# Two buffers for the combine weights of a fused attention, soft-MoE and MLP kernel, and three expert matrices loaded in halves during attention

## The chip, the cores and the metric

The kernel runs on one core of a Trainium2 chip. The metric is the device time of one execution in microseconds (us); the median of the runs shown is what a change is judged by. A core has five engines with an instruction queue each: TensorE (PE, matmuls; its weight loads are listed apart as PEld), VectorE (DVE), ScalarE (ACT), GpSimd (POOL) and SyncE (SP). Here SP issues every transfer between DRAM and on-chip memory; the transfers themselves run on the core's 16 DMA engines. Each engine takes its instructions strictly in the order in which they were written, so an instruction that waits holds up all that stands behind it on that engine.

## The reference

Three layers on 4608 tokens of width 512 (8 batches of 576 tokens, 8 heads of 64), all in fp32.

```python
# 1 attention inside chunks of 64 tokens
scores = scale * q_c @ k_c^T ; attn = softmax(scores) ; x = attn @ v_c      # -> x [4608, 512]
# 2 soft mixture of experts: 8 experts x 4 slots = 32 slots
logits = x @ phi                                    # [4608, 32]
d = softmax over the 4608 tokens ; slot_input = d.T @ x
h = relu(slot_input[e] @ w1[e]) ; slot_out[e] = h @ w2[e]    # w1[e] 512x1024, w2[e] 1024x512
c = softmax over the 32 slots                       # the combine weights
y = c @ slot_out                                    # [4608, 512]
# 3 MLP
out = softplus(y @ w_in) @ w_out                    # 512 -> 2048 -> 512
```

The kernel multiplies slot_out by w_in first (a table of 32 x 2048), so the hidden layer of the MLP is c times that table.

## The kernel before, in words

**Stages.** Attention comes first (to about 174.7 us of the profiled span). It works in 36 units, each two heads of 512 tokens: SP loads q and k of a unit (step `lq`, two transfers of 256 KB) and v for two units (`lv`, four of 128 KB), PE transposes q and k (L404), forms the scores (L435), transposes them (L468), multiplies by v (L487) and transposes the result (L522); DVE, ACT and POOL evict and scale in between. There are three buffers for q and k, so the loads of a unit are issued when the unit three before it has been transposed. Then come the experts: sixteen `H` steps of PE (L931) multiply the slot inputs by the halves of w1 (1 MB each), sixteen `SO` steps (L973) multiply by the halves of w2. Meanwhile the combine weights are prepared, and the first quarter of w_in and of w_out is converted from the words in which they are held to the number form that PE takes. Then the table is built (`Td`, L1013), and 72 quarter tiles of the MLP follow (`h` L1084, softplus on DVE and ACT, `o` L1142 to L1146) to the end.

**Combine weights.** They are made in three batches of 1536 tokens. For each: `c1` on PE transposes logits; `c20`, `c21` on DVE subtract the row maximum into a tile `cc` (L816); `c3` on ACT takes the exponential (L820); `c40` to `c42` on DVE divide by the row sum (L826 to L831); `c5` on ACT writes the high part into a tile `cr` (L839); `c6` on POOL writes the low part (L843); three `d` steps on PE transpose `cr` (L850), and three `dc` steps on DVE or ACT copy the result into the table `cT` (L856). The tiles `cc` and `cr` have one buffer each: the second batch may write `cc` only when `c6` of the first has read it. They lie where attention's expert buffers d0 to d4 were, so the first `c21` also waits for the `H` step that reads d2.

**Weight conversion.** A piece of 512 columns goes through `cb0`, `cb1`, `cb2` on DVE (L335, L338, L342), a copy and a square on ACT (L347, L350; the square lies between `cb1` and `cb2`) and a sum `cg` on POOL (L872). Pieces of w_out are then split once more (`ch` L879, `cl` L883). Four pieces of w_in and the first two of w_out stand on DVE ahead of the step `so0` (L983), which scales the first half of the experts' result; `so1` on ACT does the other half, and PE's L992 (`soT`) needs both.

**Loads.** SP's queue is in order. The sixteen halves of w1 lie in slots w0, w1, g0 to g2, d0 to d4, w2 to w6, g3 (in the order of the `H` steps); the d slots are free only when attention's buffers are closed. The halves of w2 come into i0 to i3 and w7, and then into slots that `H` or `SO` steps have left. A transfer takes one of eight semaphores in turn and waits for the transfer eight before it, so at most eight are in flight.

**Order.** A planner (`issue`) writes the instructions out. Every step has an engine, a cost, a rank and the steps and buffers that it needs; the planner keeps a clock per engine and always writes the step that could start first. Its costs set the order, not the time. Steps given the engine None cost nothing and are written as soon as what they stand behind is written. While it waits for the last two halves of w2, PE multiplies something that nothing reads (`fill`, L914).

```python
FILL = {("SO", 14): 4, ("SO", 15): 3, ("o", 0): 2}          # lost matmuls ahead of these steps
add("c21", b, ..., [("c20", b)] + start_, [("cc", b)], ...)  # takes a buffer cc
add("c6", b, ..., [("c5", b)], (), [("cc", b)], r)           # gives it back
bufs.update({"mt": 4, "cv": 4, "cc": 1, "cr": 1, ...})
```

Of the kernel before, what the change touches and what calls it, by code (L numbers as in the profile page):

```python
# [8 lines left out]
F32 = mybir.dt.float32  # L9
U32 = mybir.dt.uint32  # L10
F32R = mybir.dt.float32r
# [6 lines left out]
LAG = 3  # L18
BUSY = 36
WAIT = 0  # L20
FILL = {("SO", 14): 4, ("SO", 15): 3, ("o", 0): 2}


# [2 lines left out]
W2 = ["i0", "i1", "i2", "i3", "w7", "w0", "w1", "w2", "w3", "w4", "w5", "w6", "g3", "i0", "i1",  # L26
      "i2"]
# [117 lines left out]
def kernel(  # L145
# [12 lines left out]
    nc = tc.nc  # L158
# [127 lines left out]
    def load(nm, n, sl):  # L286


        e, i = divmod(n, 2)
        if nm == "w1":  # L290
            src = moe_w1[e].rearrange("(p k) f -> p k f", k=4)[:, 2 * i:2 * i + 2]
        elif nm == "w2":
            src = moe_w2[e, i * 512:(i + 1) * 512, :].rearrange("(p b a) f -> p b (a f)", b=2, a=2)
        else:
            src = w_out_u[256 * n:256 * n + 256, :].rearrange("(k p) f -> p k f", p=128)
        parts = halves(sl)
        if sl[0] == "w":
            for t, x in zip(parts, (src[:, 0], src[:, 1])):
                nc.sync.dma_start(out=t.bitcast(U32) if nm == "wo" else t, in_=x)
        else:  # L300
            t = V["slot", sl]
            t = (t.bitcast(U32) if nm == "wo" else t).rearrange("p (b f) -> p b f", b=2)
            for x in (slice(0, 1), slice(1, 2)) if nm == "w2" and n >= 14 else (slice(0, 2),):
                nc.sync.dma_start(out=t[:, x], in_=src[:, x])
        if nm == "w2":
            parts = [t.rearrange("p (a f) -> p a f", a=2) for t in parts]
        wt[nm, n] = parts

    def load_wi(c, pr):
        src = w_in_u[256 * pr:256 * pr + 256, 1024 * c:1024 * c + 1024].rearrange(  # L310
# [307 lines left out]
    def add(nm, key, fn, deps=(), take=(), give=(), rank=0.0, cost=None, after=()):  # L618
        s = Step(nm, key, fn, [by[d] for d in deps if d in by], take, give, rank, cost,
                 [by[d] for d in after])  # L620
        by[nm, key] = s
        steps.append(s)
# [96 lines left out]
    def at(f, *a):  # L719
        return lambda e, held: f(*a)  # L720

    for n, sl in enumerate(W1):
        if sl[0] != "d":
            add("lw", ("w1", n), at(load, "w1", n, sl), rank=100 + n)
    for n in range(5):
        add("lw", ("w2", n), at(load, "w2", n, W2[n]), rank=130 + n)
    ends = ((raw_ctx, "A1", ["d0"]), (qk_ctx, "S", ["d1", "d2"]), (v_ctx, "D", ["d3", "d4"]))
    deps = []
    for i, (c, nm, sls) in enumerate(ends):
# [79 lines left out]
    def st_c2(b, step, e, held):  # L809
        p = V["c", b]  # L810
        if step == 0:
            V["cm"] = st_p.tile([128, NC, 1], F32, tag="cm", name="cm", bufs=1)
            nc.vector.tensor_reduce(out=V["cm"], in_=p, axis=AX.X, op=ALU.max, negate=True)
        else:
            c = V["c", b] = K["keep"].tile([128, NC, NS], F32, tag="cc", name="cc")
            nc.vector.tensor_tensor(  # L816
                out=c, in0=p, in1=V["cm"].to_broadcast([128, NC, NS]), op=ALU.add)

# [16 lines left out]
        return x.unsqueeze(2).to_broadcast([128, NC, 2, NS])  # L835

    def st_c5(b, e, held):
        cr = V["cr", b] = K["keep"].tile([128, NC, 2, 2, NS], F32R, tag="cr", name="cr")
        nc.scalar.copy(out=cr[:, :, :, 0], in_=two(V["c", b]))  # L839

    def st_c6(b, e, held):
# [518 lines left out]
    held = {(sl, "w1"): 0 for sl in W1 if sl[0] != "d"}  # L1360
    held.update({(W2[n], "w2"): 0 for n in range(5)})
    bufs = {sl: 0 for sl in W1 + W2 if sl[0] != "d"}
    bufs.update({"mt": 4, "cv": 4, "cc": 1, "cr": 1, "ph": 2, "scr0": 1, "scr1": 1, "scr2": 1, "hold": 0})
    held.update({("hold", f"{j}{h}"): 2 * j + i for j in range(4) for i, h in enumerate("ab")})
    for i, k in enumerate(late):
        by["cb0", k].after = [by["o", (EARLY + 2 + 3 * i // 2, 0)]]
# [49 lines left out]
```

## Time and profile before

| | us |
|---|---|
| three runs | 678.26, 678.83, 678.56 (median 678.56) |
| the profiled execution's own time | 677.97 |
| its span, first to last instruction | 676.2 |
| attention, to the last step ahead of the experts | 174.7 |
| experts, combine weights and first conversions, to `so0` | 174.7 to 226.9 |
| table and MLP | 226.9 to 676.2 |
| busy: PE, DVE, ACT, POOL | 634.6, 430.2, 318.0, 237.8 |

The profile is of one execution, whose own time lies 1.8 above its span. A row of the timeline gives start, length, engine, line, operation, what is written from what, how many, and in brackets how long the engine stood idle before it and who released it. A row of SP's queue (SPq) gives when a transfer is issued, not when it lands. Names as trm, sops, hps and ph are PE's result tiles; g, i, w and d are weight slots.

### The profile page before, as it was taken

The page shows a single profiled execution, that of the slowest core. Times are in us where ns is not written, and L with a number is a line of the kernel's source. Part 1 is how long each engine was busy: PE and PEld are TensorE (multiplying, and loading weights), DVE is VectorE, ACT ScalarE, POOL GpSimd, SP SyncE. Part 2 cuts the span into 40 slices and gives each one's busy share as a digit, 9 for nine tenths or more (in the row PEclk, how much of TensorE's full clock was granted, in tenths as well). Part 3 has the DMA queues.
Part 4 walks back from the last instruction along what each step waited for, and adds up shares of the span by engine and source line. Part 5 has one row for each costly group of instructions (what it writes and reads, how often), then busy time and mean ns, then how long its engine had stood idle before and what let it go on. Part 6 is the DMA issues. An engine that isn't in the chain of part 4 may idle for free.

```text
span 676.2 us, 14087 instructions
## 1 busy us (share of the span) xinstructions
PE 634.6 (94%) x5849; PEld 511.6 (76%) x5849; DVE 430.2 (64%) x631; ACT 318.0 (47%) x478; POOL 237.8 (35%) x205
## 2 busy tenths in 40 slices
PE   5899899878995899999999999999999999999997
PEld 4688678756454677888788788888888888888885
DVE  1678778765237799878887877754555554545551
ACT  2566457543126587734554755544333333333330
POOL 4233233220114536613222233444433344433341
PEclk7999999998897999999999999999999999999999
DMA  9799889899999903112313510222414223231412
GB/s 169 195 245 275 234 235 287 212 300 413 416 409 411 391 5 128 59 63 93 125 63 118 195 62 32 79 78 79 110 62 125 63 85 103 78 110 63 121 35 62
DMA packets 80543, 107.93 MB, mean 160 GB/s; under 512 B 42464, under 2 KB 60896, under 8 KB 78560
## 3 DMA queue, kind: packets, MB, share of 16 engines
q1 hardware_dynamic: 80480, 107.04, 49.0%
q8 instruction: 46, 0.75, 0.5%
q14 instruction: 17, 0.14, 0.1%
HBM read 88.15 MB, written 18.87 MB: 158 GB/s over the span
## 4 chain that ended last, share of the span: by engine, by line
PE 81%; DVE 8%; issue 4%; ACT 3%; POOL 2%; DMA 1%; SPq 1%; POOLq 0%; DVEq 0%; ACTq 0%
PE trm L1146 18%; PE trm L1144 18%; PE trm L1142 18%; PE ph L1084 5%; PE tr L404 4%; PE X L487 3%; PE S L435 2%; PE hps L931 2%; PE tr L468 2%; PE tr L522 2%; PE tr L540 2%; PE tr L598 1%; DMA q<-in_q_dram 1%; DVE nm L446 1%; DVE ph L1113 1%
## 5 line engine op out<-in xcount | busy, mean ns | idle before, releaser
L1123 POOL TENSOR_TENSOR g<-hTm,g 128x1024 fp32r<-128x1024 f32 (+1 forms) x37 | 86.8, 2348 | 105.1 <-ACT g L1119 101.5
L1109 ACT ACTIVATE hTm<-hTm 128x1024 f32<-128x1024 f32 (+2 forms) x51 | 51.4, 1010 | 79.8 <-DVE hTm L1103 79.6
L1103 DVE TENSOR_SCALAR hTm<-ph 128x1024 uint32<-128x1024 uint32 (+2 forms) x51 | 59.0, 1158 | 34.6 <-PE ph L1084 34.5
L421 POOL COPY T<-T 64x512 f32<-64x512 f32 x72 | 44.0, 611 | 104.3 <-ACT T L413 103.5
L1113 DVE SCALAR_TENSOR_TENSOR hTm<-ph,hTm 128x1024 f32<-128x1024 f32 (+1 forms) x37 | 44.1, 1193 | 23.5 <-ACT hTm L1109 23.4
L1119 ACT CAST g<-hTm 128x1024 fp32r<-128x1024 f32 (+1 forms) x37 | 37.9, 1025 | 41.0 <-DVE hTm L1113 41.0
L1158 DVE TENSOR_TENSOR i<-trm,i 128x512 f32<-128x512 f32 x52 | 35.7, 686 | 32.0 <-PE trm L1146 31.8
L413 ACT COPY T<-tr 128x512 f32<-128x512 f32 x72 | 40.9, 588 | 29.5 <-PE tr L404 29.4
L1084 PEld LDWEIGHTS ph<-cT,Tc 128*128 128x128 f32 x288 | 43.6, 190 | 10.1 <-issue 2.8
L1084 PE MATMUL ph<-cT,Tc 128*128 128x256 f32 x288 | 47.0, 286 | 0.8 <-DVE ph L1113 0.7
L1103 DVE TENSOR_SCALAR siT<-ph 128x1024 uint32<-128x1024 uint32 (+1 forms) x25 | 29.5, 1180 | 26.0 <-PE ph L1084 26.0
L1123 POOL TENSOR_TENSOR g<-siT,g 128x1024 fp32r<-128x1024 f32 x12 | 28.9, 2407 | 42.8 <-ACT g L1119 42.8
L1109 ACT ACTIVATE siT<-siT 128x1024 f32<-128x1024 f32 (+1 forms) x25 | 25.7, 1026 | 36.8 <-DVE siT L1103 36.6
L1123 DVE TENSOR_TENSOR g<-ph,g 128x1024 fp32r<-128x1024 f32 (+2 forms) x27 | 29.7, 1102 | 11.9 <-ACT g L1119 11.9
L446 DVE TENSOR_REDUCE nm<-S 128x8 f32<-128x512 f32 x36 | 24.7, 686 | 18.9 <-PE S L435 18.8
L404 PE MATMUL tr<-ident,q 128*128 128x128 f32 x144 | 29.8, 290 | 6.3 <-DMA q<-in_q_dram 5.2
L1119 ACT CAST g<-ph 128x1024 fp32r<-128x1024 f32 (+2 forms) x27 | 24.9, 922 | 19.5 <-DVE ph L1113 18.1
L435 PEld LDWEIGHTS S<-T 64*64 64x64 f32 x1152 | 21.1, 137 | 16.1 <-issue 12.5
L435 PE MATMUL S<-T 64*64 64x64 f32 x1152 | 25.4, 225 | 7.5 <-issue 2.5
L404 PE MATMUL tr<-ident,k 128*128 128x128 f32 x144 | 28.9, 283 | 2.2 <-issue 2.2
L460 ACT ACTIVATE P<-P 128x512 f32<-128x512 f32 x36 | 23.0, 638 | 11.5 <-DVE P L452 11.4
L452 DVE TENSOR_TENSOR P<-S,nm 128x512 f32<-128x512 f32 x36 | 24.5, 679 | 2.1 <-PE S L435 1.3
(439 smaller groups left out, 1748.4 us busy)
## 6 DMA issues: line engine op xcount, KB each, us to landing
part<-i SPq DMA_DIRECT2D x18, 512.0 KB, 2.6
i<-part SPq DMA_DIRECT2D x18, 512.0 KB, 3.7
q<-in_q_dram SPq DMA_DIRECT2D x32, 256.0 KB, 4.7
k<-in_k_dram SPq DMA_DIRECT2D x32, 256.0 KB, 4.4
vbm<-in_v_dram SPq DMA_DIRECT2D x40, 128.0 KB, 4.2
g<-in_moe_w_dram SPq DMA_DIRECT2D x5, 1024.0 KB, 7.6
d<-in_moe_w_dram SPq DMA_DIRECT2D x5, 1024.0 KB, 12.1
i<-in_moe_w_dram SPq DMA_DIRECT2D x5, 1024.0 KB, 15.2
```

The lines of the kernel that those rows point to most:

```text
L404: nc.tensor.transpose(c, t[:, h, 2 * rr:2 * rr + 2, :].rearrange("p r d -> p (r d)"), ident)
L421: nc.gpsimd.tensor_copy(out=t[a:a + 64, :, 1], in_=t[b:b + 64, :, 2 * h])
L435: nc.tensor.matmul(out=sp[64 * o:64 * o + 64, b, 64 * i:64 * i + 64], lhsT=cs[:, 0], rhs=cs[:, 1], start=True, stop=True)
L1084: nc.tensor.matmul(out=ph(n, a, b)[:, j - a, :], lhsT=K["Tc"][:, f * 128:(f + 1) * 128], rhs=K["cT"][:, t * TT:(t + 1) * TT], start=True, ...
L1103: nc.vector.tensor_scalar(out=scratch(n, a, b).bitcast(U32), in0=ph(n, a, b).bitcast(U32), scalar1=0x80000000, scalar2=None, op0=ALU.bitwi ...
L1109: nc.scalar.activation(out=y, in_=y, func=AF.Softplus)
L1113: nc.vector.scalar_tensor_tensor(out=soft(n, a, b), in0=ph(n, a, b), scalar=0.0, in1=y, op0=ALU.max, op1=ALU.add)
L1119: nc.scalar.copy(out=V["gs", n][:, 0, a:b], in_=soft(n, a, b))
L1123: tt(e)(out=s[:, 1, a:b], in0=soft(n, a, b), in1=s[:, 0, a:b].bitcast(F32), op=ALU.subtract)
L1142: nc.tensor.matmul(out=po, lhsT=s[:, 0, j, ts_], rhs=wr[:, hs], start=(n in begin and j == 0), stop=False)
L1144: nc.tensor.matmul(out=po, lhsT=s[:, 0, j, ts_], rhs=wr[:, ls], start=False, stop=False)
L1146: nc.tensor.matmul(out=po, lhsT=s[:, 1, j, ts_], rhs=wr[:, hs], start=False, stop=(j == 3 and n in finish))
```

## The change

Two things are edited. The tiles `cc` and `cr` get two buffers each. And three halves of w1, number 10, 11 and 12 of the `H` steps (slots w2, w3, w4), are no longer loaded after attention's last loads but in six parts of 512 KB, each written into SP's queue right behind the q and k loads of one unit: units 8, 10, 12, 21, 26 and 31. The old load steps stay in the planner as empty ones, so that it plans as before. The same is done with the first five halves of w2 (i0 to i3, w7): they now stand in the queue right behind the load of g3, ahead of d0 to d4 instead of behind them.

```diff
+EARLY_LOADS = {10: (8, 10), 11: (12, 21), 12: (26, 31)}
...
+    def load_half(n, sl, i):
+        src = moe_w1[n // 2].rearrange("(p k) f -> p k f", k=4)[:, 2 * (n % 2) + i]
+        if i == 0:
+            wt["w1", n] = halves(sl)
+        nc.sync.dma_start(out=wt["w1", n][i], in_=src)
...
+    def ahead(key, f, step):
+        add("ld", key, f, cost={None: 0.0}, after=[step])
+
     for n, sl in enumerate(W1):
         if sl[0] != "d":
-            add("lw", ("w1", n), at(load, "w1", n, sl), rank=100 + n)
+            add("lw", ("w1", n), at(lambda: None) if n in EARLY_LOADS else at(load, "w1", n, sl),
+                rank=100 + n)
+        for i, u in enumerate(EARLY_LOADS.get(n, ())):
+            ahead((n, i), at(load_half, n, sl, i), ("lq", u))
     for n in range(5):
-        add("lw", ("w2", n), at(load, "w2", n, W2[n]), rank=130 + n)
+        add("lw", ("w2", n), at(lambda: None), rank=130 + n)
+        ahead(("w2", n), at(load, "w2", n, W2[n]), ("lw", ("w1", 15)))
...
-            c = V["c", b] = K["keep"].tile([128, NC, NS], F32, tag="cc", name="cc")
+            c = V["c", b] = K["keep"].tile([128, NC, NS], F32, tag=f"cc{held['cc', b]}", name="cc")
...
-        cr = V["cr", b] = K["keep"].tile([128, NC, 2, 2, NS], F32R, tag="cr", name="cr")
+        cr = V["cr", b] = K["keep"].tile(
+            [128, NC, 2, 2, NS], F32R, tag=f"cr{held['cr', b]}", name="cr")
...
-    bufs.update({"mt": 4, "cv": 4, "cc": 1, "cr": 1, "ph": 2, "scr0": 1, "scr1": 1, "scr2": 1, "hold": 0})
+    bufs.update({"mt": 4, "cv": 4, "cc": 2, "cr": 2, "ph": 2, "scr0": 1, "scr1": 1, "scr2": 1, "hold": 0})
```

On SP, in attention, the loads of units 8 to 10 stand so before (q and k of a unit, then v; the numbers are those of the tiles):

```order
L265 DMA q_586<-in_q_dram 128x2x256
L265 DMA k_587<-in_k_dram 128x2x256
L265 DMA q_634<-in_q_dram 128x2x256
L265 DMA k_635<-in_k_dram 128x2x256
L272 DMA vbm_115<-in_v_dram 128x4x64 x4
L265 DMA q_733<-in_q_dram 128x2x256
L265 DMA k_734<-in_k_dram 128x2x256
L265 DMA q_768<-in_q_dram 128x2x256
```

On SP, at the same place, now (w2a and w2b are the two parts of w1's half number 10):

```order
L266 DMA q_586<-in_q_dram 128x2x256
L266 DMA k_587<-in_k_dram 128x2x256
L314 DMA w2a_590<-in_moe_w1_dram 128x1024
L266 DMA q_637<-in_q_dram 128x2x256
L266 DMA k_638<-in_k_dram 128x2x256
L273 DMA vbm_115<-in_v_dram 128x4x64 x4
L266 DMA q_736<-in_q_dram 128x2x256
L266 DMA k_737<-in_k_dram 128x2x256
L314 DMA w2b_591<-in_moe_w1_dram 128x1024
L266 DMA q_772<-in_q_dram 128x2x256
```

A part of 512 KB stands between the loads of one unit and those of the next; w3a follows two units later, w3b behind unit 21, w4a behind 26, w4b behind 31, and the six are gone from the queue after attention.

On DVE, in the experts' stage, the first two batches of combine weights stand so before (trm_3387 is the first batch's `c1`, trm_3393 the second's; ts is the eviction of the experts' hidden layer, rz a reciprocal):

```order
L816 TENSOR_TENSOR cc<-trm_3387,cm 128x384
L813 TENSOR_REDUCE cm<-trm_3393 128x12
L826 TENSOR_REDUCE cs<-cc 128x12
L828 TENSOR_SCALAR cs<-cs 128x12
L829 RECIPROCAL cs<-cs 128x12
L831 TENSOR_TENSOR cc<-cc,cs 128x384
L949 COPY ts<-hps 128x256
L904 TENSOR_SCALAR rz<-trm_3491 128x1
L905 RECIPROCAL rz<-rz 128x1
L816 TENSOR_TENSOR cc<-trm_3393,cm 128x384
```

On DVE, at the same place, now (trm_3399 is the third batch):

```order
L830 TENSOR_TENSOR cc<-trm_3387,cm 128x384
L827 TENSOR_REDUCE cm<-trm_3393 128x12
L840 TENSOR_REDUCE cs<-cc 128x12
L830 TENSOR_TENSOR cc<-trm_3393,cm 128x384
L842 TENSOR_SCALAR cs<-cs 128x12
L843 RECIPROCAL cs<-cs 128x12
L827 TENSOR_REDUCE cm<-trm_3399 128x12
L845 TENSOR_TENSOR cc<-cc,cs 128x384
L840 TENSOR_REDUCE cs<-cc 128x12
L842 TENSOR_SCALAR cs<-cs 128x12
L843 RECIPROCAL cs<-cs 128x12
L964 COPY ts<-hps 128x256
```

The second batch's subtraction has moved ahead of the eviction ts; its division follows right behind rz, and then the third batch's subtraction and division, which before stood among the conversions of w_in. Two `dc` copies stand between that division and the first `cb0`, and one more behind the first `cb1`.

On PE, between the `SO` steps on the slots w3 and w4, before (trm from cr are the `d` steps of the third batch):

```order
L973 MATMUL sops_3360<-w3a,hTm 32x256 x2
L973 MATMUL sops_3361<-w3a,hTm 32x256 x2
L973 MATMUL sops_3360<-w3b,hTm 32x256 x2
L973 MATMUL sops_3361<-w3b,hTm 32x256 x2
L850 MATMUL trm_3686<-ident,cr 128x128 x4
L850 MATMUL trm_3692<-ident,cr 128x128 x4
L850 MATMUL trm_3700<-ident,cr 128x128 x4
L973 MATMUL sops_3360<-w4a,hTm 32x256 x2
```

On PE, from behind the step on w0, now (the first transpose belongs to the first batch, the next three to the second, the last three to the third):

```order
L865 MATMUL trm_3600<-ident,cr 128x128 x4
L865 MATMUL trm_3605<-ident,cr 128x128 x4
L865 MATMUL trm_3611<-ident,cr 128x128 x4
L988 MATMUL sops_3360<-w1a,hTm 32x256 x2
L988 MATMUL sops_3361<-w1a,hTm 32x256 x2
L988 MATMUL sops_3360<-w1b,hTm 32x256 x2
L988 MATMUL sops_3361<-w1b,hTm 32x256 x2
L865 MATMUL trm_3631<-ident,cr 128x128 x4
L865 MATMUL trm_3640<-ident,cr 128x128 x4
L865 MATMUL trm_3650<-ident,cr 128x128 x4
L865 MATMUL trm_3657<-ident,cr 128x128 x4
L988 MATMUL sops_3360<-w2a,hTm 32x256 x2
```

The `d` steps have moved one batch ahead: those of the third batch stand where the second's stood (ahead of w2), and from w2 to the fill matmuls no `d` step is left between the `SO` steps.

## Rows read from the trace of the kernel before

**Rows 1.** PE, timeline (start, us, engine, line, what, count, idle before), 205 to 232 us.
```profile
205.06 1.53 PE L850 MATMUL trm<-ident,cr 128*128 128x128 f32 x12 [2.37 <-POOL cr L843]
...
213.20 2.82 PE L850 MATMUL trm<-ident,cr 128*128 128x128 f32 x12 [4.72 <-POOL cr L843]
...
221.29 1.99 PE L914 MATMUL hps<-acc,ident 128*128 128x256 f32 x8
...
225.72 1.08 PE L973 MATMUL sops<-i,hTm 128*32 128x256 f32 x16
227.40 1.16 PE L992 MATMUL trm<-rep,ts 128*128 128x128 f32 x8 [0.59 <-DVE ts L983]
229.19 2.89 PE L1013 MATMUL trm<-g,soT 128*128 128x128 f32 x16 [0.63 <-DVE soT L999]
```

**Rows 2.** SP's queue, timeline, the last parts of w2.
```profile
208.68 4.14 SPq L304 DMA_DIRECT2D i<-in_moe_w_dram  x4
```

**Rows 3.** Landing, transfers issued 208.6 to 212.9: KB each, us to landing.
```profile
i<-in_moe_w_dram SPq DMA_DIRECT2D x4, 512.0 KB, 12.7
```

**Rows 4.** Windows: us, busy (count) of PE, PEld, DVE, ACT, POOL; clock; DMA share; GB/s.
```profile
33.00:50.00 17.00, 16.82 (x407) 14.30 (x408) 12.63 (x29) 11.40 (x24) 6.11 (x10) 1.00 0.93 238
208.00:213.00 5.00, 0.48 (x12) 0.00 (x0) 4.19 (x8) 3.86 (x5) 2.95 (x2) 0.79 1.04 414
213.00:217.00 4.00, 3.80 (x24) 3.04 (x28) 3.05 (x6) 2.14 (x4) 2.26 (x3) 0.50 1.00 409
235.00:260.00 25.00, 23.93 (x113) 19.39 (x112) 24.21 (x38) 20.91 (x35) 10.48 (x9) 1.00 0.11 40
260.00:676.00 416.00, 411.27 (x1932) 339.80 (x1931) 259.79 (x279) 182.98 (x210) 156.93 (x80) 1.00 0.27 88
```

**Rows 5.** POOL, timeline, low parts of the second and third batch.
```profile
203.20 1.80 POOL L843 TENSOR_TENSOR cr<-cc,cr 128x768 fp32r<-128x768 f32 x1 [12.04 <-ACT cr L839]
...
211.34 1.81 POOL L843 TENSOR_TENSOR cr<-cc,cr 128x768 fp32r<-128x768 f32 x1 [1.86 <-issue]
```

**Rows 6.** DVE, timeline, 205 to 227 us.
```profile
205.04 0.56 DVE L816 TENSOR_TENSOR cc<-trm,cm 128x384 f32<-128x384 f32 x1 [7.42 <-POOL cr L843]
...
206.83 0.55 DVE L826 TENSOR_REDUCE cs<-cc 128x12 f32<-128x384 f32 x1
207.43 0.69 DVE L342 SCALAR_TENSOR_TENSOR cvt<-g,cvt 128x512 f32<-128x512 f32 x1
...
208.50 1.40 DVE L831 TENSOR_TENSOR cc<-cc,cs 128x384 f32<-128x384 f32 x1
...
211.91 1.78 DVE L342 SCALAR_TENSOR_TENSOR cvt<-g,cvt 128x512 f32<-128x512 f32 x1 [0.74 <-ACT g L350]
...
215.21 0.69 DVE L856 CAST cT<-trm 128x512 fp32r<-128x512 f32 x1 [0.91 <-PE trm L850]
...
220.37 1.68 DVE L338 SCALAR_TENSOR_TENSOR cvt<-w0a,cvt 128x512 uint32<-128x512 uint32 x1
...
224.84 0.97 DVE L342 SCALAR_TENSOR_TENSOR cvt<-w0b,cvt 128x512 f32<-128x512 f32 x1 [0.75 <-ACT w0b L350]
226.86 0.48 DVE L983 TENSOR_SCALAR ts<-sops,rz 128x256 f32<-128x256 f32 x1 [1.05 <-PE sops L973]
```

**Rows 7.** SP's queue, timeline, the k load of unit 15.
```profile
58.46 0.42 SPq L265 DMA_DIRECT2D k<-in_k_dram  x1
```

**Rows 8.** Landing of that load: KB, us to landing.
```profile
k<-in_k_dram SPq DMA_DIRECT2D x1, 256.0 KB, 5.2
```

**Rows 9.** PE, timeline, the first transposes of unit 15.
```profile
64.39 0.38 PE L404 MATMUL tr<-ident,q 128*128 128x128 f32 x2
```

**Rows 10.** The instructions on the slots d0 to d4: min/median/max ns, first and last start.
```profile
L931 PE MATMUL hps<-d,siT x40: 592/592/593, 182.8 to 186.6; 128*32 128x512 f32 x40
L304 SPq DMA_DIRECT2D d<-in_moe_w_dram x5: 327/328/1068, 153.8 to 165.2; - x5
...
DMA to landing us min/median/max: 9.6/12.1/14.2
```

## The prediction

> **What bounds the kernel now.** I read the windows by stage first. From 260 us to the end PE is busy in 411.27 of 416 us, and in 235 to 260 in 23.93 of 25 [rows 4]: once the MLP runs, PE sets the end, and the change leaves those matmuls alone. So the end moves by as much as the start of the table and the MLP, and that start hangs on `so0`, the DVE step at 226.86 [rows 6].
>
> Then the timelines of PE and DVE and the landings, for what `so0` waits for. Three chains end close together. PE: the last `SO` step starts at 225.72 and takes 1.08 [rows 1]. Transfers: the last four parts of w2 are issued until 208.68 + 4.14 = 212.8, the last of them some 0.3 before that, and land 12.7 after their issue [rows 2, 3], the last at 225.2, half a microsecond ahead of that step. DVE: its last conversion ends at 224.84 + 0.97 = 225.81, and it stands idle 1.05 before `so0` [rows 6]. So transfers end last, and DVE is 1 us behind them. The two waits of PE for `c6` on POOL, 2.37 at 205.06 and 4.72 at 213.20 [rows 1], don't reach the end: after them PE multiplies fill (1.99 at 221.29) while it waits for w2.
>
> **Part 1, the transfers.** While weights load the 16 DMA engines move 414 GB/s at a share of 1.04 [rows 4], so a part of 512 KB takes 1.27 us. Six parts fewer after attention are 7.6 us: w2's last part lands at 217.6 instead of 225.2, as long as the engines stay busy. They do: i0 to i3 and w7 (5 MB) now fill the time in which SP waits for attention's buffers. The price of that order is that d0 to d4 come behind 5 MB instead of behind 3, 2 MB or 5.1 us later. The last was issued at 165.2 and landed at most 14.2 later [rows 10], so at most at 184.5; the last eight of the forty matmuls that read these slots start from about 185.8 (the last at 186.6). PE's `H` steps hide it, with 1.3 us to spare in the worst case; beyond that every microsecond would be a microsecond of `H`.
>
> **Part 2, PE without the waits.** With two buffers the second batch's `c6` no longer holds the third. The first `c21` still waits for `H` to leave d2, and the third batch's `c5` stands on ACT behind a copy of the first batch's last `d` step, which PE reaches at the same time as before. So the third `c6` runs where the second ran, 203.20 to 205.0 [rows 5], and its `d` steps start at 205.06 where the second's did: a short wait there stays, the one of 4.72 goes. Seven `SO` steps at about 0.9 (1.08 with the tail) bring PE to 212.9, fill to 214.9, the next step and its fill to 217.3, and the last step, half a microsecond after its data, ends at 219.2: 7.6 earlier than now.
>
> **Part 3, DVE, which doesn't follow all the way.** DVE ends its conversions at 225.81 and does them in order. Out of that stretch go the third batch's sum (0.55 at 206.83) and division (1.40 at 208.50), the collision of a conversion with the third `c6` (1.78 instead of 0.69, [rows 5, 6]: 1.09), and one copy with the wait before it (0.69 + 0.91 at 215.21): 4.64. The stretch begins no earlier: the first `cb1` now meets the POOL operation that ends at 205.0, and the copies of the `d` steps come at 206, as now, so `cb2` stands near 207.4 again. In comes one more collision: the second and third `cb2` now follow each other, and POOL's `cg` of the one starts as the other wants to; price 1.68 - 0.69 = 1.0, as in the row at 220.37. So the last conversion ends at 225.81 - 4.6 + 1.0 = 222.2, and `so0` starts at 222.3, gain 4.5. Bounds: 2.5, if two such collisions more come in; 7.6, if DVE is done before PE.
>
> **Part 4, what is late next: PE stands idle ahead of `so0`.** From 219.2 to the end of `so0` (222.3 + 0.48) it has 3.6 us without work, where now it has 0.59 [rows 1]. Before the transposes at 213.20 it had been busy for 0.48 of 5 us; the granted clock was 0.79 in that stretch and 0.50, 1.2 GHz, in the next four [rows 4], and twelve transposes took 2.82. After the wait of 2.37 the same twelve took 1.53 [rows 1]. My 3.6 lies between the two. Behind it stand 1.16 (L992) and 2.89 (L1013), 4.05 us at 2.4 GHz; at 1.2 they take 2.82 / 1.53 = 1.84 times as long, 3.4 more. Bounds 0 and 3.4; I take 2.0, since the idle time is nearer to the 4.72. The Trainium skill (TensorE: Matmul & The Clock Gate, HAM oscillation — how this bites in real kernels) says that matmuls in bursts with waits for data between them start at the low clock after every wait. By that rule the whole 3.4 would be paid; the row at 213.20 bears it out, the one at 205.06 does not.
>
> **Part 5, the six loads in attention.** They cost nothing where the DMA engines have gaps and the q and k that follow have time. No gain is possible: nothing that attention needs comes sooner. The tightest unit that I found is 15: its k is issued at 58.46, lands 5.2 later at 63.7 [rows 7, 8], and PE transposes that unit's q from 64.39 [rows 9]: 0.7 to spare. Three parts, 3.8 us, now stand ahead of it from 34 us on, and the engines' share in 33 to 50 is 0.93 [rows 4], a gap of 1.2. So 3.8 - 1.2 - 0.7 = 1.9 is the most that it can come late if no later gap helps; the other three parts stand farther apart. Bounds 0 and all 7.6; I take 0.5, near to what unit 15 allows when the time from 50 to 58 has gaps too.
>
> **Sum.** -4.5 (part 3, the smaller of the two gains) + 2.0 (part 4) + 0.5 (part 5) = -2.0. The profiled execution took 677.97, so 676.0; the median of the runs shown lies 0.6 above it, so 676.6.
>
> **Rivals.**
>
> *All of it arrives.* If POOL's operations and DVE's fall beside each other, DVE is done at 219 and PE waits for nothing: -7.6 + 0.5, so 671.5. For it: not every conversion is stretched, the one at 207.43 took 0.69 [rows 6]. Against it: four `cg` and two further POOL operations still stand between them, and DVE has one more step in each piece that waits for ACT's square. The Trainium skill (DMA: Bandwidth & Descriptors, Rules for kernel authors) says to issue a transfer early, compute, and wait for it late; by that rule the 7.6 would all be hidden and this would be the result. Chance 0.12.
>
> *Nothing arrives.* Part 3 at its lower bound: -2.5 + 2.0 + 0.5 = 0, so 678.6; or part 4 at its upper bound: -4.5 + 3.4 + 0.5 = -0.6, so 678.0. For it: in 235 to 260 DVE is busy 24.21 of 25 us [rows 4], so a start of PE that comes sooner may meet a DVE that doesn't. Against it: the same conversions are also done sooner. Chance 0.25.
>
> *Slower: q and k come too late.* The parts stand ahead of q and k in the same queue, and 0.7 us to spare is little. If the three parts ahead of unit 15 make PE wait 1.9 there and the three later ones as much again, attention ends 3.8 to 4.5 later; with part 3 at its lower bound and part 4 as taken that is -2.5 + 2.0 + 4.2 = +3.7, with the forecast's own -4.5 it is +1.7: 680.3 to 682.3. It decides from 2.5 us of delay on (no gain left) and is slower beyond what can be told from 3.9. Against it: a DMA share of 0.93 leaves gaps, and PE has idle time of its own in attention that takes up part. Chance 0.13.
>
> **How the numbers follow.** The forecast has 0.50; its own range is 674.5 to 678.0 (part 3 from -6 to -3, parts 4 and 5 within their bounds but not all at one end). A measurement of this kernel can tell about 0.2%, 1.4 us, from no change: faster is below 677.2, slower above 679.9. Faster: 0.45 of the forecast, 0.12 of the first rival, 0.03 of the second, 0.60. Within: 0.05 of the forecast and 0.22 of the second rival, 0.27. Slower: the third, 0.13. The range 672.5 to 679.8 leaves out half of the first rival and most of the third.
>
> **What would show it.** In the changed profile: (1) w2's last part lands near 217.6, and the last `SO` step ends near 219. (2) Only one wait for `c6` of more than 1 us on PE, near 205. (3) `so0` starts near 222.3 right behind a conversion on DVE, not behind PE. (4) PE idle some 3.6 us before L992, and the granted clock at 0.50 for part of what follows. (5) The last step of attention within 1 us of 174.7. The prediction is wrong if `so0` is released by PE (part 3 too pessimistic), if attention ends 2 us later or more (part 5), or if the MLP takes longer than the 449.3 us from 226.9 to the end by much more than the 2.0 of part 4.

## The result and the profile after

The change makes the kernel slower. Its median is 685.6 us (680.9 to 691.7, 13 runs) against 678.8 (677.2 to 685.2) of the kernel before beside it; the ratio is 1.0092, 95% interval 1.0065 to 1.012, about 6 us. The forecast was 676.6, so its sign was wrong. The profiled execution of after is the second longest of its 13: its own time is 689.9 and its span 688.2, where before had 676.2. A second profile of the same kernel (run e9 below) has a span of 680.4, from the shortest of its six runs; both are read here, because the distance between them is part of the finding.

Windows first: the stretches that answer to [rows 4], and attention from 20 us to the start of its last `X` matmul (columns as in [rows 4]). After:

```profile
20.00:183.86 163.86, 134.11 (x3081) 110.01 (x3080) 108.16 (x241) 83.53 (x178) 40.70 (x67) 0.96 0.87 253
33.00:50.00 17.00, 14.93 (x313) 12.26 (x310) 11.12 (x24) 10.88 (x23) 6.10 (x10) 1.00 0.96 257
247.00:272.00 25.00, 23.92 (x113) 19.36 (x112) 24.23 (x38) 20.89 (x35) 10.54 (x9) 1.00 0.10 33
272.00:688.00 416.00, 411.25 (x1932) 339.80 (x1930) 259.94 (x279) 183.00 (x210) 156.89 (x80) 1.00 0.28 88
```

And before, the same work of attention:

```profile
20.00:164.47 144.47, 128.26 (x3086) 106.47 (x3083) 108.53 (x242) 83.74 (x179) 40.94 (x67) 0.99 0.89 262
```

Shifted by 12 us, the MLP is the same to a tenth of a microsecond (411.25 against 411.27 of PE in 416). All the time is lost in attention: its last `X` starts 19.4 us later, and some 8 us of that are won back before `so0`. DVE, ACT and POOL have the same busy times in both rows; PE has 5.9 us more for the same matmuls, and 13.5 us more idle time (163.86 - 134.11 against 144.47 - 128.26).

What that idle time waits for, by the view of PE's waits over the same stretch (us in total, times, longest). Before:

```profile
PE tr L404 <- issue: 3.2, 2, 2.2
PE S L435 <- issue: 2.5, 1, 2.5
PE X L487 <- issue: 2.3, 2, 1.7
PE tr L540 <- issue: 1.4, 1, 1.4
```

After:

```profile
PE S L442 <- issue: 8.9, 4, 3.5
PE X L494 <- issue: 6.2, 4, 2.1
PE tr L547 <- issue: 3.6, 3, 2.1
PE tr L529 <- issue: 3.2, 2, 2.9
PE S L442 <- DVE P L459: 1.8, 4, 0.7
PE tr L529 <- DVE x L517: 1.2, 3, 0.5
PE tr L411 <- issue: 1.0, 1, 1.0
```

"Issue" is time in which PE waits for nothing that the profile shows: 9.4 us in six pauses before, 22.9 in fourteen after. The difference, 13.5, is all of the new idle time. No row of after names a transfer of q or k. The timeline of PE shows such a pause (start, us, engine, line, what, count, idle before):

```profile
47.99 0.33 PE L442 MATMUL S<-T 64*64 64x64 f32 x5
51.79 1.00 PE L442 MATMUL S<-T 64*64 64x64 f32 x26 [3.47 <-issue]
```

It lies in the middle of one unit's score matmuls, whose operands have all been there since the first of them. The reading is that PE has run out of instructions. They come by DMA too: the view of the DMA queues shows packets of kind "instruction" of 16 KB, 24 of them in the stretch above. In the window 49.30 to 50.40 of after (queue, kind: packets, MB, share):

```profile
q1 hardware_dynamic: 847, 0.21, 99.9%
q8 instruction: 1, 0.02, 5.8%
```

The packet runs from 49.34 to 50.35; PE starts again 1.44 us after its end. That is so for each of the 111 pauses put down to issue between 20 and 190 us in the fourteen profiles of this study: PE resumes 1.19 to 1.63 us after the end of such a packet. And PE stands still for such a packet more often while weights are under way. Between 20 us and the issue of attention's last load the fourteen traces have 294 of these packets. Of the 140 that moved while a weight transfer had been issued and had not landed, 53 were followed by a pause; of the other 154, 18. The Trainium skill (Runtime: NRT & Kernel Launch, Instruction fetch mechanics) says that an engine's sequencer fetches its instructions through a DMA queue of its own in blocks of 16 KiB, and that the cost is mostly hidden. The size agrees with the trace; hidden it is not here.

The pause has a sequel. The windows of 2 us around it (the clock is the third figure from the end):

```profile
48.00:50.00 2.00, 0.32 (x6) 0.18 (x5) 0.69 (x1) 0.32 (x1) 1.11 (x2) 1.00 1.18 277
50.00:52.00 2.00, 0.21 (x8) 0.21 (x12) 0.00 (x0) 0.00 (x0) 0.00 (x0) 0.96 0.43 76
52.00:54.00 2.00, 2.00 (x61) 1.88 (x58) 0.86 (x2) 0.00 (x0) 0.00 (x0) 0.50 0.81 261
54.00:56.00 2.00, 2.00 (x40) 1.80 (x38) 1.36 (x3) 0.97 (x2) 0.00 (x0) 0.69 0.92 174
```

After 3.5 us without work the granted clock is 0.50, 1.2 GHz, in the next window and 0.69 in the one behind it. It falls so four times in this stretch, each time within 2.1 us behind a pause of 2.1 to 3.5 us. Not every pause of that length has it: behind this one of 2.9 us the clock stays at 1.00.

```profile
77.19 0.38 PE L529 MATMUL tr<-ident,x 128*128 128x128 f32 x2 [2.90 <-issue]
```

```profile
70.00:80.00 10.00, 6.99 (x212) 5.78 (x214) 6.25 (x13) 4.25 (x9) 2.44 (x4) 1.00 0.98 254
80.00:90.00 10.00, 8.57 (x169) 6.74 (x159) 7.47 (x20) 6.60 (x15) 2.85 (x5) 1.00 0.90 279
```

Over the whole stretch the clock is 0.96, against 0.99 before. As an estimate from these two means, 0.04 of 163.86 us against 0.01 of 144.47, that is 5.1 us, most of PE's 5.9 us more.

What follows attention. The last v load of attention is issued at 160.25, within the first of these rows of SP's queue, and at 140.69 before; w2's last four parts come in the second:

```profile
157.15 4.60 SPq L273 DMA_DIRECT2D vb<-in_v_dram  x3
...
220.52 4.14 SPq L305 DMA_DIRECT2D i<-in_moe_w_dram  x4
```

They land 12.6 us after their issue (12.7 in [rows 3]), the last at 237.01. From the last v load to that landing it is 76.8 us, and was 84.5 before: the six parts fewer are worth the 7.7 us, but they are counted from a start that lies 19.6 us later. The rows of PE that answer to [rows 1], and the end of DVE's that answer to [rows 6]:

```profile
216.78 1.53 PE L865 MATMUL trm<-ident,cr 128*128 128x128 f32 x12
...
220.82 1.53 PE L865 MATMUL trm<-ident,cr 128*128 128x128 f32 x12 [0.92 <-POOL cr L858]
...
236.96 1.15 PE L988 MATMUL sops<-i,hTm 128*32 128x256 f32 x16
238.91 1.13 PE L1007 MATMUL trm<-rep,ts 128*128 128x128 f32 x8 [0.80 <-ACT ts L1001]
240.58 2.86 PE L1028 MATMUL trm<-g,soT 128*128 128x128 f32 x16 [0.54 <-DVE soT L1014]
```

```profile
237.43 0.94 DVE L349 SCALAR_TENSOR_TENSOR cvt<-w0b,cvt 128x512 f32<-128x512 f32 x1 [0.77 <-ACT w0b L357]
238.29 0.47 DVE L998 TENSOR_SCALAR ts<-sops,rz 128x256 f32<-128x256 f32 x1
```

The two waits for `c6` of [rows 1], 7.1 us, are down to 0.92. `so0` stands at 238.29, 11.4 later than before, and from it to the end it is 449.9 us against 449.3.

### The profile page after: what moved, and what is told of

It is laid out like the page before. It is cut to its first block, busy times and chain, and to the rows that moved or that the text cites. A ratio compares the mean times of both kernels' runs of the same rounds, so it can differ in the third digit from the quotient of the medians.

```text
span 688.2 us, 14098 instructions
## 1 busy us (share of the span) xinstructions
PE 637.4 (93%) x5849; PEld 513.3 (75%) x5849; DVE 434.8 (63%) x634; ACT 316.2 (46%) x475; POOL 237.6 (35%) x205
## 4 chain that ended last, share of the span: by engine, by line
PE 81%; DVE 7%; issue 5%; DMA 3%; ACT 2%; POOL 1%; SPq 1%; POOLq 0%; DVEq 0%
PE trm L1161 18%; PE trm L1159 18%; PE trm L1157 18%; PE ph L1099 5%; PE tr L411 4%; PE X L494 3%; PE S L442 3%; PE tr L475 2%; PE tr L529 2%; PE hps L946 2%; PE tr L547 2%; PE sops L988 1%; DMA w1a<-in_moe_w_out_dram 1%; PE tr L605 1%; DMA q<-in_q_dram 1%
## 5 line engine op out<-in xcount | busy, mean ns | idle before, releaser
L1138 DVE TENSOR_TENSOR g<-ph,g 128x1024 fp32r<-128x1024 f32 (+2 forms) x27 | 29.7, 1104 | 11.9 <-ACT g L1134 11.8
L467 ACT ACTIVATE P<-P 128x512 f32<-128x512 f32 x36 | 22.8, 636 | 11.4 <-DVE P L459 11.4
L529 PE MATMUL tr<-ident,x 128*128 128x128 f32 x144 | 23.4, 285 | 4.8 <-issue 3.2
## 6 DMA issues: line engine op xcount, KB each, us to landing
i<-in_moe_w_dram SPq DMA_DIRECT2D x5, 1024.0 KB, 14.2
```

Of the source, the lines that this page charges most:

```text
L1138: tt(e)(out=s[:, 1, a:b], in0=soft(n, a, b), in1=s[:, 0, a:b].bitcast(F32), op=ALU.subtract)
```

## The experiments

Two theories stood at first. F: the weights' bytes delay PE's instruction fetches, PE pauses, and its clock falls. Q: the halves stand ahead of q and k in SP's queue, which come late (the forecast's slower rival). Others were added as they arose. Every run is told by its ratio to the kernel before beside it, whose median was 678.8 beside after, 678.2 beside e1 to e4, 677.8 beside e5 to e8 and 676.4 beside e9 to e12: times from different sets are compared by their ratios. All times in us; "length" is from 20 us to the start of the last `X` in the profiled run, "PE busy", "issue" (PE's pauses put down to issue) and the waits are PE's in that stretch; "load" is the issue of attention's last load, "w2" the landing of w2's last part.

| kernel | ratio [95%] | median | length | PE busy | issue | waits for q, k, v | load | w2 | so0 |
|---|---|---|---|---|---|---|---|---|---|
| before | 1 | 678.8 | 144.5 | 128.3 | 9.4 | 0 | 140.7 | 225.2 | 226.9 |
| after | 1.0092 [1.0065, 1.012] | 685.6 | 163.9 | 134.1 | 22.9 | 0 | 160.3 | 237.0 | 238.3 |
| e9 after again | 1.0108 [1.0063, 1.0152] | 683.8 | 156.1 | 133.8 | 12.6 | 1.6 | 152.8 | 228.6 | 230.5 |
| e1 no early | 1.002 [0.9991, 1.0049] | 680.2 | 143.1 | 128.2 | 7.5 | 0.3 | 141.4 | 224.6 | 228.2 |
| e2 early only | 1.0144 [1.0102, 1.0185] | 687.7 | 158.5 | 134.3 | 13.1 | 2.5 | 155.3 | 236.9 | 240.3 |
| e3 tiny | 1.0053 [1.0026, 1.0079] | 681.9 | 150.7 | 129.6 | 14.2 | 0.2 | 145.6 | 229.1 | 230.2 |
| e4 quarters | 1.0051 [1.0024, 1.0078] | 681.7 | 151.9 | 130.1 | 13.2 | 1.6 | 149.2 | 227.9 | 231.3 |
| e5 none | 1.008 [1.0045, 1.0114] | 684.3 | 137.2 | 126.5 | 3.1 | 0 | 137.9 | 233.1 | 234.2 |
| e6 spread | 0.9989 [0.9964, 1.0015] | 677.3 | 150.7 | 129.7 | 11.1 | 0.2 | 144.8 | 227.5 | 228.6 |
| e7 spread, 8 | 0.9998 [0.9967, 1.0028] | 677.7 | 147.0 | 128.3 | 6.9 | 3.3 | 147.1 | 222.9 | 224.1 |
| e8 pairs | 1.0041 [1.0008, 1.0075] | 682.1 | 154.5 | 133.6 | 11.4 | 2.6 | 149.3 | 229.2 | 231.9 |
| e10 even | 1.0042 [1.0004, 1.0079] | 680.4 | 150.1 | 130.6 | 10.5 | 1.1 | 148.0 | 224.3 | 226.2 |
| e11 fine | 1.0018 [0.9988, 1.0048] | 678.2 | 146.5 | 128.5 | 9.2 | 0.5 | 141.1 | 225.0 | 226.1 |
| e12 one buffer | 1.0056 [1.0026, 1.0086] | 680.8 | 150.9 | 132.4 | 9.5 | 1.9 | 146.4 | 223.5 | 230.2 |

One profile stands for each kernel, and executions of one kernel differ by several us; the ratios carry the verdicts, the profiles show how. From `so0` to the end it is 448.9 to 450.6 in all of them.

**e1, without the early halves.**

```diff
-EARLY_LOADS = {10: (8, 10), 11: (12, 21), 12: (26, 31)}
+EARLY_LOADS = {}
```

> The changed kernel without the six early halves: the three matrices load behind attention again, the two buffers each and the new place of i0 to i3 and w7 stay. Theory F (the halves lengthen attention because bytes queued on the DMA engines delay PE's instruction fetches, so that PE stands still in the middle of steps): attention is that of before, PE's pauses put down to issue between 20 and 185 us sum to about 11 us and not to 23; as the transfers behind attention are as many as before, w2's last part lands near 225 and so0 gains at most 1 us: 677.5 to 679. Rival Q (the halves stand ahead of q and k, which come late): the same time, but with no fewer pauses of that kind. Rival B (the two buffers and the new order cost the time, not the halves): still about 685.

It is 680.2, a little above what was expected, and cannot be told from before. The loss goes with the halves: not B. PE's pauses are 7.5 us, fewer even than F had it (8.6 up to 185 us, where F said about 11), and so Q, which expected no fewer of them, misses:

```profile
20.00:163.09 143.09, 128.17 (x3080) 106.03 (x3080) 107.65 (x241) 83.30 (x178) 40.43 (x67) 0.99 0.91 262
```

But e1 has a cost that after hasn't. The `H` steps wait for the loads of d0 to d4, which now stand behind those of w2's first five halves and here behind the six parts as well (in before no `H` step waits for them):

```profile
PE hps L946 <- DMA d<-in_moe_w_dram: 4.1, 3, 1.4
```

`H` ends at 198.0, in before at 192.4, and `so0` comes 3.6 us after w2's landing, behind DVE's conversions. So what the two buffers bring can't be read from e1, and e1's time is not a clean price of attention alone.

**e2, the early halves alone.** The tags `cc` and `cr` have one buffer again, and the first five of w2 load at their old place.

```diff
-"cc": 2, "cr": 2
+"cc": 1, "cr": 1
```

> The six early halves alone: one buffer each for the combine weights' steps, i0 to i3 and w7 at their old place. Theory F and rival Q: attention is as late as in the changed kernel, the six parts fewer behind it give some 7.6 us back on the transfers, and the two waits for c6 may keep a part of that from so0: 684 to 688, with PE's pauses put down to issue near 20 us or more by F and near 11 with waits for q and k by Q. Rival B: 677 to 679.

687.7, at the upper end for F and Q. Attention is 15 us longer than in e1. Both causes are seen, pauses at issue of 13.1 us (F expected 20) and waits for q and k of 2.5 (Q's), and PE is busy 6 us longer. By the ratios e2 is 0.5% slower than after, but the intervals overlap: that the rest of the change is worth something is likely from this run, not shown by it.

**e3, six small transfers in the same places.** The matrices load whole behind attention.

```diff
-        nc.sync.dma_start(out=wt["w1", n][i], in_=src)
+        nc.sync.dma_start(out=halves(sl)[i][:, 0:128], in_=src[:, 0:128])
```

> The changed kernel, but the six early transfers carry only the first 128 of 1024 columns (64 KB each instead of 512), and the whole matrices are loaded behind attention as before: the same number of transfers at the same places of the queue with an eighth of the bytes. Theory F: the bytes are the cost, so the time is that of the kernel without early halves within 1.5 us, about 677.5 to 680. Rival P (the place in the queue is the cost: each further transfer takes one of the eight that may be under way and a turn of SP): about as late in attention as the changed kernel, and without its six parts fewer behind it, so 688 to 693.

681.9, far from P's 688 to 693: the place in the queue does not make the whole loss. It is 1.7 above e1, a little more than F allowed, and these two intervals overlap. But at 1.0053 it is clear of before, so with an eighth of the bytes about half of the loss may be left. Its profile has one pause of 4.4 us and 14.2 in all, which F did not expect; with one profile that may be chance. Whether the place has a share stays open. That the number of transfers alone makes it is unlikely: e11 below puts forty into attention, at 1.0018, and issues its last load there at 141.1, before at 140.7.

**e4, the three added matrices in quarters.**

```diff
-EARLY_LOADS = {10: (8, 10), 11: (12, 21), 12: (26, 31)}
+EARLY_LOADS = {10: (8, 9, 10, 11), 11: (12, 14, 20, 22), 12: (25, 27, 30, 32)}
+        c = slice(512 * (i % 2), 512 * (i % 2) + 512)   # 256 KB a part
```

> The changed kernel with the same 3 MB in twelve transfers of 256 KB, each behind q and k of a unit of its own (8 to 11, 12, 14, 20, 22, 25, 27, 30, 32). Theory F: the bytes are the same, but less of them is queued at a time when a fetch comes; a part of the loss goes: 680 to 684, and PE's pauses put down to issue between 11 and 23 us. Rival Q: 1.27 us of delay at a unit becomes 0.6, inside the 0.7 that the tightest unit has: nearly all of the loss goes, 675 to 678. Rival P (number of transfers): more loss than the changed kernel, 688 or more.

681.7: within F, outside Q and P. Parts of half the size, at more units, cost about half by the ratios (1.0051 against 1.0092), though the intervals overlap a little.

**e5, no expert weights in attention at all.** All matrices of w1 stand behind the last q, k and v.

```diff
-            add("lw", ("w1", n), ..., rank=100 + n)
+            add("lw", ("w1", n), ..., rank=100 + n, after=[("lq", 35), ("lv", 17)])
```

> No expert weights during attention at all: the kernel without early halves (680.2 beside a before of 678.2, PE's pauses put down to issue 8.6 us), with its other five matrices (5 MB, ten parts of 512 KB) behind attention's last q, k and v too. Theory F (bytes queued on the DMA engines delay PE's instruction fetches): the pauses fall below 5 us and attention ends 3 to 8 us earlier; the transfers behind it, which set so0, have ten parts more, 12.7 us, so 685 to 690. Rival T (the pauses come with q, k and v, or are chance): pauses as before, attention ends where it did, 692 to 694.

684.3, a little better than F's 685 to 690, and far from T's 692 to 694 (counted from w2's landing in e1, 224.6 + 12.7, T would still give some 690). This is the run that tells most, though with one profile. Attention is 6 us shorter than in e1, PE's pauses go from 7.5 to 3.1 us, its clock stays at 1.00, its busy time falls by 1.7; w2's last part lands 8.5 later than in e1, since ten parts of 1.27 us have moved behind attention, whose last load comes 3.5 earlier:

```profile
20.00:157.16 137.16, 126.47 (x3083) 104.89 (x3084) 108.14 (x242) 83.29 (x179) 40.89 (x67) 1.00 0.83 232
```

```profile
PE X L494 <- issue: 1.8, 2, 1.3
PE tr L411 <- issue: 1.3, 1, 1.3
```

So weights' bytes delay the fetches without the early halves too. With this edit the planner also writes the `H` steps on d0 to d4 behind all others; so it does in e6, e7, e11 and e12.

**e6 and e7, everything in quarters, one behind each unit.** Five matrices behind units 9 to 28 (e6), or eight behind units 4 to 35 (e7); the others behind attention.

```diff
+EARLY_LOADS = {n: range(9 + 4 * n, 13 + 4 * n) for n in range(5)}                                # e6
+EARLY_LOADS = {n: range(4 + 4 * i, 8 + 4 * i) for i, n in enumerate((0, 1, 2, 3, 4, 10, 11, 12))}  # e7
```

> The kernel without early halves, its five matrices that load during attention cut into twenty parts of 256 KB, one each behind q and k of units 9 to 28, where before they came as two times two halves of 512 KB and three times 1 MB at once. The bytes are the same. Theory F with depth (a fetch waits for what is queued at that moment): pauses below 8.6 us, attention 1 to 5 us shorter, and as the transfers behind it are the same, 675 to 679. Rival S (only the sum of bytes counts): 680 within 1.5.

> All eight matrices of the changed kernel's attention in parts of 256 KB, one each behind q and k of units 4 to 35. Theory F with depth: below the 681.7 of the kernel that cuts only the three added matrices, 677 to 681. Rival S: the bytes of the changed kernel, so its time, about 684 to 686; and if every part costs more than the 0.64 us that it saves behind attention, slower than the same with five matrices.

Both come out where F with depth put them: 677.3 and 677.7. Against after, e7 moves the same 8 MB in attention, and its interval lies wholly below: how the bytes are cut and spread decides, not their sum (not S). (That e7 has another order of `H` doesn't explain it, as `H` waits for no load in after.) Against e1, e6 gains 0.3% by the ratios, but those intervals overlap, and its profile has more pauses than e1's (11.1 against 7.5, in a run at the upper end of its twelve; attention 7.6 us longer and not 1 to 5 shorter), so for e6 the mechanism is not shown; its `H` steps no longer wait for d0 to d4, which may be all of the gain. Nor is e7 free in attention: in its profile the last load goes out 6.4 us later than before, and the six parts fewer behind it pay for that. Neither beats before by what can be told.

**e8 and e10, the six halves at other units.**

```diff
-EARLY_LOADS = {10: (8, 10), 11: (12, 21), 12: (26, 31)}
+EARLY_LOADS = {10: (9, 9), 11: (17, 17), 12: (28, 28)}      # e8
+EARLY_LOADS = {10: (9, 13), 11: (17, 21), 12: (25, 29)}     # e10
```

> The changed kernel with the same six halves in three pairs, each matrix at once, behind q and k of units 9, 17 and 28. Theory F with depth: 1 MB at a time delays a fetch that meets it longer, so no better than the changed kernel: 684 to 690, with single pauses of 3 us or more. Rival N (each disturbance costs the same, whatever its size): three in place of six, 681 to 683.

> The changed kernel with its six halves at even distances, behind q and k of units 9, 13, 17, 21, 25 and 29, in place of 8, 10, 12, 21, 26 and 31. If the bunch at 8, 10 and 12 makes the loss, 680 to 682.5; if the size of a part does (512 KB against 256), the time of the changed kernel within 1.5 us.

682.1 and 680.4, both at 1.004. Even distances take away about half of the loss, as expected of the bunch, and so do the pairs, though both intervals overlap that of after. The pairs are against depth as it was put: 1 MB at once should have been no better than the halves of after. They fit rival N. Which units are bad ones, and why, stays open.

**e9, the changed kernel again**, beside the same before as e10.

> The changed kernel once more, beside the same before as the kernels with other places for the parts. If the three pairs (ratio 1.004) are really better than its six halves (1.009), it stays at 684 or more; if the two differ by chance alone, it comes out between 681.5 and 684. Theory F (instruction fetches of PE delayed by the weights' bytes): its profile has pauses put down to issue of 10 to 23 us between 20 us and attention's last X step, and each ends 1.2 to 1.6 us behind an instruction packet of 16 KB.

It is 683.8, which by the words of the expectation is within what chance would give (681.5 to 684). But that range was set beside a before of 677.8, and here before is 676.4: the ratio is 1.0108, after 1.0092 in the first set. Beside two kernels at 1.004 the difference is hardly chance, though the intervals still overlap a little. The profile, of the shortest of its six runs, shows attention 11.6 us longer than before in place of 19.4:

```profile
20.00:176.09 156.09, 133.78 (x3084) 108.66 (x3083) 108.44 (x242) 84.04 (x179) 41.02 (x67) 0.97 0.91 265
```

Its parts are others than in the first profile. The pauses are 12.6 us, only 3.2 more than before. PE is busy 5.5 longer; the clock fell three times, each time within 2.4 us of the end of a pause of 1.9 to 2.3. Waits for q and k are 1.6, and 1.3 are smaller waits. Each pause ends 1.3 to 1.6 us behind an instruction packet, as expected.

**e11, five matrices in forty parts of 128 KB**, behind units 4 to 35 and eight loads of v.

```diff
+AT = sorted([(u, "lq", u) for u in range(4, 36)] + [(2 * p + 0.5, "lv", p) for p in range(6, 14)])
+EARLY_LOADS = {n: [x[1:] for x in AT[8 * n:8 * n + 8]] for n in range(5)}
```

> Five matrices during attention in forty parts of 128 KB, behind q and k of units 4 to 35 and behind eight loads of v, where the kernel with parts of 256 KB took 677.3. Theory F with depth: again shallower, 674.5 to 677, with fewer pauses than 8 us. If the depth no longer matters, or forty transfers cost more turns of the queue than they save, 677 to 680.

678.2, and 9.2 us of pauses, in the second of the two ranges: parts below 256 KB bring nothing more that can be told.

**e12, e7 with one buffer each** (the edit of e2's diff), to price parts 2 and 3 of the forecast where attention isn't in the way.

> All eight matrices in parts of 256 KB over units 4 to 35 (677.7), but one buffer each for the combine weights' steps. It prices parts 2 and 3 of the forecast where attention isn't lengthened. If the forecast's count holds (4.6 us of DVE work go from the stretch ahead of so0, 1.0 come), so0 and the end come 2 to 4 us later: 679.5 to 682. If the transfers alone set so0, 677.7 within 1.

680.8, in the range of the forecast's count and 3.1 above e7; by the ratios it is 0.6%, and the two intervals just meet (1.0028 and 1.0026). One buffer gives the long wait back. PE in e12:

```profile
210.10 1.53 PE L866 MATMUL trm<-ident,cr 128*128 128x128 f32 x12 [1.79 <-POOL cr L859]
218.75 1.97 PE L866 MATMUL trm<-ident,cr 128*128 128x128 f32 x8 [4.36 <-POOL cr L859]
...
229.04 1.08 PE L989 MATMUL sops<-i,hTm 128*32 128x256 f32 x16
```

and in e7:

```profile
210.53 1.09 PE L866 MATMUL trm<-ident,cr 128*128 128x128 f32 x8 [1.84 <-POOL cr L859]
...
222.88 1.14 PE L989 MATMUL sops<-i,hTm 128*32 128x256 f32 x16
```

w2's last part lands at 223.5 in the one and 222.9 in the other; with one buffer the last `SO` step starts 5.5 us after that and `so0`, at 230.18, 6.7, where in e7 `so0` follows the landing by 1.2.

## Why the prediction was wrong, point by point

**Part 5 is the step that failed.** It put the six loads in attention at 0.5 us, with bounds of 0 and 7.6. Measured, attention's last load is issued 19.6 us later in one profile of after and 12.1 in the other (152.8 against 140.7). Both lie outside the bounds. The bounds were worked out from one mechanism, that q and k come late for PE; a transfer was thought to cost at most its own time, and only in what waits for it. What happened is that PE, which waits for q and k next to nothing there (0 us in after, 1.6 in e9), stops for its own instructions, which come through the same DMA engines, and goes on at the low clock after some of these stops. In after that is 13.5 us of pauses and 5.9 of longer work, all of the 19.4; in e9 3.2 and 5.5 of 11.6. e1 shows that the six halves do this (7.5 us of pauses without them, and no loss that can be told); e5, and the count of late packets with and without weights under way, show that weights' bytes do. The trace of before held the hint: the four rows of PE's pauses shown above, up to 2.5 us each, had no counterpart among the forecast's terms.

**Part 1** had the size right and the start wrong. Six parts fewer take 7.7 us off the way from attention's last load to w2's last landing (84.5 to 76.8; 83.2 in e1 to 75.8 in e9). But since the DMA engines are full from there on (a share of 0.99 to 1.02 in after's windows from 162 to 232 us), all of it starts with attention's last load, and every microsecond by which that comes later is lost whole: -7.7 + 19.6 = +11.9, and w2 lands 11.85 later. That the later d loads are hidden held in after, where no row of `H` waits for a transfer; but there attention ended late. In e1, where it ended as before and the six parts stood ahead of them as well, `H` waited 4.1 us for them, so the forecast's 1.3 us to spare were not put to the test.

**Part 2** held in kind: one wait for `c6`, 0.92, instead of 2.37 and 4.72.

**Part 3** held in size, where it could act. The count of the forecast gives 4.6 - 1.0 = 3.6 for two buffers; e12 against e7 is 3.1 by the medians and 0.6%, 3.9, by the ratios. The forecast's gain of 4.5 is this 3.6 and the 1.05 that DVE stood idle ahead of `so0` [rows 6]; it needed transfers that land sooner, and in after they land later. With transfers, PE and DVE as in e7 the three end within 1.3 us of each other (222.9, 224.0, 224.2), and DVE is not 3 us behind.

**Part 4** was too much: 2.0 forecast, 0.5 measured (449.9 against 449.3 from `so0` to the end). PE stands idle for 0.80 ahead of L1007, not for 3.6, as PE and DVE end together. The slow clock of [rows 4] turned up elsewhere, in attention.

**The sum.** With measured terms the profiled run comes out: w2 11.85 later, `so0` 0.4 nearer to it, 0.5 in the MLP, 12.0 of span. e9 by the same account: w2 lands 3.4 later, `so0` 3.7, and the span is 4.2 longer.

**The slower rival** had the right side, with 0.13, and the wrong mechanism: waits for q, k and v are 0 to 3.3 us in all runs, and largest in e7, which is not slow. Its 680.3 to 682.3 falls short of 685.6. Of the five signs, the second and third came in kind, not at their times (no wait for `c6` above 0.92, `so0` right behind a conversion at 238.29); the first, fourth and fifth did not. What it named as a sign that part 5 is wrong, attention 2 us later or more, came.

**What stays open.** The trace shows when an instruction packet is moved, not when it was asked for, so how long it waits behind data was not measured by itself. Why the clock falls behind some pauses and not behind others was not tried. And six halves cost 0.4% in two sets of places and 1% in another, at the same bytes; no run says which property of the place does it.

## What to carry to other kernels

Read the pauses "from issue" on an engine with many small instructions, above all those in the middle of a step: when an instruction packet ends just before each, the engine is starved of instructions, and any transfer added there can cost far more than its own time. A load moved into a stretch whose DMA share looks like 0.9 is not free because nobody waits for it; try it whole, in small parts spread evenly, and not at all, and take the one that gives the shortest sum of attention and of the transfers behind it.

## What was not expected of the hardware

PE executes some 6,200 matmuls and weight loads in attention's 144 us and takes a 16 KB packet of instructions about every 6 us there. How often such a packet is late goes with the weights under way: 4 pauses (4.2 us) between 20 and 190 us in e5, which loads no weights in attention, 7 (11.1) in before, 14 (22.9) and 9 (12.6) in the two profiles of after. Behind a pause of 3.5 us the granted clock was also 0.50 in the next window of 2 us, behind one of 2.9 it stayed at 1.00. The spread of the times tells nothing of this: the eight runs of e5 lie within 3.1 us of each other, but so do the six of e9, and the thirteen of after within 10.8.
